# Top-32 attention without two small VectorE steps: eight entries written by GpSimd, scores three tiles ahead, operand splits spread

## The chip, the core and the metric

The kernel runs on one core of a Trainium2 chip. The time is device time in microseconds, taken from the first to the last instruction of the program; the median of several runs counts. The core has five engines that each work through their own instructions in order: TensorE (PE, with its weight loads as PEld), VectorE (DVE), ScalarE (ACT), GpSimd (POOL) and SyncE (SP), which here only issues DMAs. They wait for each other through semaphores.

## The reference

The attention has 4 x 8 heads of 576 rows and 64 columns. In each row of scores only those at or above the 32nd largest take part in the softmax:

```
scores = scale * q @ k.T                      # scale = 1/8
kth    = np.partition(scores, -32)[..., -32:-31]
scores = np.where(scores >= kth, scores, -1e9)
attn   = exp(scores - max); attn /= sum + 1e-9
out    = attn @ v
```

Its output, as 2304 tokens of 512, goes through a soft mixture of experts (`_moe_ref`: 8 experts with 4 slots each) and a top-2 mixture of experts (`_moe2_ref`: 8 experts). Both have weights of 512 x 1024 and 1024 x 512 per expert, all in float32.

## The kernel before

Two heads form a pair; there are 16 pairs. The 2 x 576 rows of a pair are nine tiles of 128 rows: four of the first head (t = 0 to 3), one with the last 64 rows of both (t = 4), four of the second head (t = 5 to 8). That makes 144 tiles. `attention` is one loop over steps `i`; in each step every engine gets one stage of several tiles, so that a tile passes through the engines over about ten steps:

- `score` (PE, then ACT): the 576 scores of each row from `QS` and `KS` into PSUM tile `S`, copied by ACT (L479) into `SS[i]`. It runs two tiles ahead of DVE's step. A pair of tiles shares one of five buffers `s`, which is ten tiles.
- `steps` (DVE): seven MAX8 over 82 columns each (L497) leave 56 candidates `C`. For the tile before, three MAX8 (L500) and two MATCH_REPLACE8 (L502) bring the 24 largest candidates into `MX`; L504 multiplies the 24th by a little less than one into `PB`.
- `count` (ACT, L517): `g`, the sign of `PB` minus the score, and its sum over the row, `SM`. So the kernel knows how many scores lie above the 24th candidate.
- `under` (POOL, L523): `u = g * s`, the scores below the bound with positive sign. Behind them `u` has nine entries that DVE writes in `fill` (L529) from `fewer`, `SM` and the 24th value: these stand for the scores above, as many as are wanted for the eighth of the following MAX8 to be the 32nd of the row.
- `pick` (DVE, L534): MAX8 over `u`; its eighth value, in `TH`, is the threshold.
- `mask` (ACT L540, then POOL L541): a relu of threshold minus score, and the row's largest minus the score, in place.
- `soft1` (PE L546, L547; ACT L553, L558): transposes of both, the second multiplied by a very large number, so that the exponential (ACT) of what is masked is zero. Every second tile also does the fifth, shared key chunk (`misc`, `et2`).
- `soft2` (PE L568, L569): the weights times `V` with a column of ones, accumulated in PSUM tile `av`. For t = 4 this runs twice with all 128 columns, once for each head. `finish` (DVE L581 to L586) divides by the sum; its pieces wait in the list `fins` and are taken between the MAX8s of the next steps.

`QS` and `KS` hold each operand as a high part, rounded to what the fast matmul takes, and a low part. For the next pair these come from `raw` (one DMA of 608 KB, `load`, L413): `split` (POOL L431, L433) makes both parts in `hl`, and `stack` lays them out in `QS` and `KS` by DMA (L437). The splits are four POOL instructions of 576 or 640 columns, one in each of four steps in a row. `raw` has two buffers, `hl` one. The first pair takes its scores straight from unsplit operands.

Table `post` names what is issued at the end of a step, `aux` (the transposes `xtr`, the `logit` and its parts, of the mixture that follows) what goes between the stages of a step. In `post` stand the loads, the stacks, and the first expert weights: five of 2 MB each at steps 40, 56, 72, 88 and 104 (`more`), and half of one at 120. Each engine's order is the order in which the program is written; SP runs ahead of the others as far as its waits let it.

After the attention the mixtures follow: matmuls on expert weights, whose buffers are filled anew as soon as the matmuls on the old content are done.

Of the kernel before, what the change touches and what calls it, by code (L numbers as in the profile page):

```python
# [8 lines left out]
F32 = mybir.dt.float32  # L9
# [9 lines left out]
UNDER = 1.0 - 2.0 ** -24  # L19
# [20 lines left out]
def moe_after_topk_attention(ctx: ExitStack, tc: tile.TileContext, q, k, v, phi, w1, w2, wg, wn, noise, u1, u2, qk, vt, out):  # L40
# [7 lines left out]
    dram = pool("dram", space=DRAM)  # L48
    wa = pool("wa")
    wz = pool("wz").tile([128, 2048], F32, name="wz")  # L50
# [36 lines left out]
    fewer = const.tile([128, 3, 4], F32, name="fewer")  # L87
    G.iota(fewer, pattern=[[-6, 3], [-2, 4]], base=528, channel_multiplier=0, allow_small_or_imprecise_dtypes=True)
    SM, PB = (const.tile([128, NT], F32, name=x) for x in ("SM", "PB"))

    TH = const.tile([128, NT + 8], F32, name="TH")
# [24 lines left out]
    def wload(i):  # L116
# [9 lines left out]
        n = 4 if m == 3 else 1  # L126
        d = WT[m, e].rearrange("p (c f) -> p c f", c=c)
        s = (w1, w2, u1, u2)[m][e].rearrange("(c p) f -> p c f", p=128)
        for a in range(n):
            cs = slice(a * c // n, (a + 1) * c // n)  # L130
            nc.sync.dma_start(d[:, cs], s[:, cs])
# [22 lines left out]
    ohw, ng = (x.rearrange("p (t e) -> p t e", e=8) for x in (TH[:, 0:NT], PB))  # L154
# [205 lines left out]
    def attention(st):  # L360
# [27 lines left out]
        RAW, HL, SP, SS, MX, G1, UU, AP, ET, E2, AV, C = ({} for _ in range(12))  # L388
        post, aux, fins, splits, cur = {}, {}, [], [], [0]
# [32 lines left out]
        def halves_of(j, a):  # L422
            splits.extend([(j, a, 0), (j, a, 1)])

        def split(j, a, l):
            if a == 0 and l == 0:
                HL[j] = tr.tile([128, 2, S + KW], F32R, name="hl")
            c = slice(S * a, S + KW * a)
            x, r = HL[j][:, :, c], RAW[j][:, c]
            if l == 0:  # L430
                G.tensor_scalar(x[:, 0], r, 1.0, 0.0, op0=OP.mult, op1=OP.add)  # L431
            else:
                G.tensor_tensor(x[:, 1], r, x[:, 0], op=OP.subtract)  # L433

        def stack(j, h):
            def move(o, i):
                nc.sync.dma_start(o.bitcast(F32), i.bitcast(F32))  # L437
            x = HL[j][64 * h:64 * h + 64]
            for l in range(2):
                o, r = QS[h][64 * l:64 * l + 64], x[:, l, 0:S]  # L440
# [5 lines left out]
            for z in range(2):  # L446
                move(KS[h][64 * z:64 * z + 64], x[:, :, S:])

        def score(i):
# [25 lines left out]
            if p is None:  # L475
                for hf in range(2):
                    A.copy(s[:, 288 * hf:288 * hf + 288], ph[hf][:, :288])
            else:
                A.copy(s.rearrange("p (a b) -> p a b", a=2), p[:, :, :288])  # L479
# [8 lines left out]
        def steps(i):  # L488
# [1040 lines left out]
```

## Time and profile before

| | us |
|---|---|
| median of 3 runs | 779.21 (779.13 to 779.62) |
| profiled execution | 783.5 |
| its span, first to last instruction | 781.6 |
| busy: PE, DVE, ACT, POOL | 755.3, 591.3, 490.3, 485.2 |

The busy times are over the whole span. Attention is the first part of it, up to about 440 us: there DVE, ACT and POOL are busy nearly all the time, and afterwards much less. A matmul's end is modelled, and the durations of neighbours on one engine overlap, so two starts in a row tell more than a duration. In the chain of work that ended last PE has 65% and DVE 22% of the span.

### The profile page before, as it was taken

Reading aid. Unit: us, or ns where it says so; the run is one execution under the profiler, and the core shown is the slowest. Engines: PE = TensorE matmul, PEld = TensorE weight load, DVE = VectorE, ACT = ScalarE, POOL = GpSimd, SP = SyncE. Lnnn points to the kernel's source line nnn. Section 1 sums busy time; section 2 is a strip of 40 time slices with the busy share of each in tenths; the row PEclk is TensorE's granted clock in tenths of the full one; section 3 lists DMA queues with packets and bytes.
Section 4 is the critical chain, followed back from the end, with each engine's and each line's share of the span. In section 5 each row is a group of like instructions: output and inputs, shape, how many; then the busy total and the mean of one; then the engine's idle time right before and its main releaser. Section 6 shows DMA issues by size and latency. Waiting matters only on the chain.

```text
span 781.6 us, 17123 instructions
## 1 busy us (share of the span) xinstructions
PE 755.3 (97%) x5623; PEld 628.0 (80%) x5623; DVE 591.3 (76%) x2916; ACT 490.3 (63%) x1019; POOL 485.2 (62%) x475
## 2 busy tenths in 40 slices
PE   9999999999999999899999999879999999999996
PEld 4799999898999889898989743356886788888884
DVE  4999999999999999889999330794654555565551
ACT  2999999999999999789998410582231322222221
POOL 3899888977898788689877200455726064273043
PEclk9999999999999999989999999898999999999998
DMA  4456878475474754755385879886955898254145
GB/s 155 115 123 169 216 196 222 89 222 136 107 213 107 186 157 97 215 129 147 65 223 205 300 279 400 274 314 214 332 157 65 291 284 188 40 67 70 16 63 68
DMA packets 62085, 135.21 MB, mean 173 GB/s; under 512 B 12450, under 2 KB 13090, under 8 KB 61986
## 3 DMA queue, kind: packets, MB, share of 16 engines
q1 hardware_dynamic: 54946, 123.83, 53.4%
q0 software_dynamic: 7040, 10.18, 9.4%
q8 instruction: 46, 0.75, 0.4%
q14 instruction: 53, 0.43, 0.2%
HBM read 84.37 MB, written 17.97 MB: 131 GB/s over the span
## 4 chain that ended last, share of the span: by engine, by line
PE 65%; DVE 22%; ACT 4%; DMA 3%; POOL 2%; issue 2%; SPq 0%; POOLq 0%; ACTq 0%; DVEq 0%
PE av L568 9%; PE acc L1286 9%; PE acc L1288 9%; PE acc L1287 9%; DVE c L497 7%; PE S L461 6%; PE st L546 4%; DVE TH L534 4%; DVE c L502 3%; PE av L569 3%; DVE mx L500 3%; PE hp L1262 2%; DMA wx<-in_moe_w_dram 2%; PE st L547 2%; PE acc L825 2%
## 5 line engine op out<-in xcount | busy, mean ns | idle before, releaser
L497 DVE MAX8 c<-s 128x8 f32<-128x82 f32 (+1 forms) x1008 | 222.9, 230 | 15.0 <-ACT s L479 7.7
L523 POOL TENSOR_TENSOR u<-g,s 128x576 f32<-128x576 bf16 x144 | 185.9, 1291 | 18.1 <-ACT g L517 11.4
L568 PE MATMUL av<-vb,et 128*128 128x65 f32 x1280 | 163.0, 271 | 0.0
L568 PEld LDWEIGHTS av<-vb,et 128*128 128x128 f32 x1280 | 159.8, 193 | 0.5 <-issue 0.4
L541 POOL TENSOR_SCALAR s<-s,mx 128x576 f32<-128x576 f32 x144 | 107.9, 749 | 55.0 <-ACT a L540 28.3
L1298 POOL DMA_INDIRECT out_dram<-y,ii x40 | 65.1, 1628 | 120.7 <-ACT y L1297 61.0
L1267 ACT ACTIVATE hh<-hp 128x640 fp32r<-128x640 f32 x62 | 43.7, 704 | 136.4 <-PE hp L1262 109.3
L1286 PE MATMUL acc<-wh,hh 128*128 128x512 f32 x320 | 127.8, 399 | 0.6 <-DVE hl L1268 0.6
L1288 PE MATMUL acc<-wh,hl 128*128 128x512 f32 x320 | 125.9, 393 | 0.0
L1287 PE MATMUL acc<-wl,hh 128*128 128x512 f32 x320 | 125.6, 393 | 0.0
L1268 DVE SCALAR_TENSOR_TENSOR hl<-hp,hh 128x640 fp32r<-128x640 f32 x62 | 51.1, 824 | 90.0 <-ACT hh L1267 89.2
L517 ACT ACTIVATE g<-s,PB 128x576 bf16<-128x576 f32 x144 | 112.6, 782 | 8.3 <-DVE PB L504 3.5
L546 PE MATMUL st<-identf,s 128*128 128x128 f32 x576 | 115.0, 280 | 1.3 <-POOL s L541 1.3
L461 PE MATMUL S<-ks,qs 128*128 128x288 f32 x600 | 114.6, 317 | 1.1 <-ACT s L479 1.1
L540 ACT ACTIVATE a<-s,TH 128x576 bf16<-128x576 f32 x144 | 114.9, 798 | 0.0
L534 DVE MAX8 TH<-u 128x8 f32<-128x585 f32 x144 | 109.4, 760 | 1.9 <-POOL u L523 1.8
L547 PE MATMUL st<-steep,a 128*128 128x128 bf16 x576 | 106.0, 220 | 0.0
L479 ACT COPY s<-S 128x576 f32<-128x576 f32 x141 | 91.4, 648 | 12.3 <-PE S L461 6.8
L461 PEld LDWEIGHTS S<-ks,qs 128*128 128x128 f32 x600 | 85.1, 191 | 9.2 <-ACT et L553 2.5
L546 PEld LDWEIGHTS st<-identf,s 128*128 128x128 f32 x576 | 84.9, 147 | 8.6 <-POOL s L541 2.2
L558 ACT ACTIVATE et<-st 128x512 f32<-128x512 f32 x144 | 85.7, 595 | 7.3 <-PE st L547 7.1
L500 DVE MAX8 mx<-c 128x8 f32<-128x56 f32 x432 | 86.3, 200 | 0.1
(341 smaller groups left out, 1263.5 us busy)
## 6 DMA issues: line engine op xcount, KB each, us to landing
wa<-in_moe_w_dram SPq DMA_DIRECT2D x11, 2048.0 KB
ks<-hl SPq DMA_DIRECT2D x60, 320.0 KB
wb<-in_moe_w_dram SPq DMA_DIRECT2D x5, 2048.0 KB
raw<-in_qk_dram SPq DMA_DIRECT2D x15, 608.0 KB
wy<-in_moe_w_dram SPq DMA_DIRECT2D x4, 2048.0 KB
wa<-in_moe_w_dram SPq DMA_DIRECT2D x16, 512.0 KB
wb<-in_moe_w_dram SPq DMA_DIRECT2D x16, 512.0 KB
vb<-in_vt_dram SPq DMA_DIRECT2D x16, 390.0 KB
```

Of the source, the lines that this page charges most:

```text
L461: T.matmul(ph[hf][:, :288], QS[h][:, q0:q0 + 128], KS[h][:, l, ks], start=(n == 0), stop=(n == len(mm) - 1))
L497: V.max(C[i][:, c * 8:c * 8 + 8], SS[i][:, cut[c]:cut[c + 1]])
L517: A.activation(g, SS[i], AF.Sign, bias=PB[:, i:i + 1], scale=-UNDER, accum_out=SM[:, i:i + 1])
L523: G.tensor_tensor(u[:, 0:S], G1[i], SS[i], op=OP.mult)
L534: V.max(thr(i, 8), UU[i])
L540: A.activation(AP[i // 2][:, S * (i % 2):S * (i % 2) + S], SS[i], AF.Relu, bias=thr(i), scale=-1.0)
L546: T.matmul(o, SP[i // 2][:, ks], identf, start=True, stop=True, is_transpose=True)
L547: T.matmul(o, AP[i // 2][:, ks], steep, start=False, stop=True, skip_group_check=True)
L568: T.matmul(o, ET[i][:, c], VB[j % 2][:, h, c], start=(c == 0), stop=False, skip_group_check=True)
L1286: T.matmul(ACC[j], HH[n][:, r], WH[n], start=(c == 0), stop=False)
L1287: T.matmul(ACC[j], HH[n][:, r], WL[n], start=False, stop=False)
L1288: T.matmul(ACC[j], HL[n][:, r], WH[n], start=False, stop=(c == 7))
```

## The change

It has eight parts, all in or around `attention`:

- L504 goes. `count` takes the 24th value itself as its bias, with a scale a little over one instead. The third MAX8 of the candidates writes its eight values straight into the table `T24`; `MX` keeps sixteen.
- L529 goes. POOL writes eight entries behind `u`, `fewer` minus `SM`, in an instruction of its own right behind `under`. These entries now are whole numbers and not multiples of the 24th value; so that they stay above or below all scores, the scores are scaled by 2 to the -40 when ACT copies them, and the exponential's scale takes it back. `pick` reads 584 columns.
- `score` runs three tiles ahead, and stands ahead of `aux` in a step.
- The splits of a pair are two instructions of 608 columns (high part) and four of 304 (low part), in six of nine steps, from 7 steps ahead of the previous pair's first tile. The low part is written over `raw`; `hl` holds the high part alone and has two buffers. The stack of `KS` takes four DMAs for a head instead of two. The stack of the first head is issued two steps earlier.
- At t = 4 `soft2` uses 64 columns of the weights for each head, on the two halves of the array (`tile_position`), into two `av` tiles that are made once and zeroed where t = 4 lies.
- `finish` is put into its list one step later, and so is `xtr`.
- The five first expert weights come in quarters of 512 KB, at steps 40 + 9i + 0, 1, 2 and 4; the half weight at step 86.
- The check of whether the fast way holds has one more condition.

```diff
-                MX[i] = wm.tile([128, 24], F32, name="mx", bufs=6)
+                MX[i] = wm.tile([128, 16], F32, name="mx", bufs=6)
...
-                    if c in (0, 2, 4):
+                    if c in (0, 2):
                         V.max(MX[k][:, c * 4:c * 4 + 8], C[k])
+                    elif c == 4:
+                        V.max(last8(T24, k), C[k])
...
-                    elif c == 5:
-                        V.tensor_scalar(PB[:, k:k + 1], MX[k][:, 23:24], UNDER, None, op0=OP.mult)
-                if 0 <= i - LP < NT:
-                    if c == CP - 2:
-                        fill(i - LP)
-                    elif c == CP:
-                        pick(i - LP)
+                if 0 <= i - LP < NT and c == CP:
+                    pick(i - LP)
...
-            A.activation(g, SS[i], AF.Sign, bias=PB[:, i:i + 1], scale=-UNDER, accum_out=SM[:, i:i + 1])
+            A.activation(g, SS[i], AF.Sign, bias=last8(T24, i, 1), scale=-OVER, accum_out=SM[:, i:i + 1])
...
-            u = UU[i] = wt.tile([128, S + 9], F32, name="u", bufs=2)
+            u = UU[i] = wt.tile([128, S + 8], F32, name="u", bufs=2)
             G.tensor_tensor(u[:, 0:S], G1[i], SS[i], op=OP.mult)
+            G.tensor_tensor(u[:, S:S + 8], fewer, SM[:, i:i + 1].to_broadcast([128, 8]), op=OP.subtract)
...
-                A.copy(s.rearrange("p (a b) -> p a b", a=2), p[:, :, :288])
+                A.activation(s.rearrange("p (a b) -> p a b", a=2), p[:, :, :288], AF.Copy, scale=TINY)
...
-                HL[j] = tr.tile([128, 2, S + KW], F32R, name="hl")
...
+                HL[j] = tr.tile([128, W], F32R, name="hl", bufs=2)
+            f = slice(a * W // n, (a + 1) * W // n)
+            r, x = RAW[j][:, f], HL[j][:, f]
             if l == 0:
+                G.tensor_scalar(x, r, 1.0, 0.0, op0=OP.mult, op1=OP.add)
             else:
+                G.tensor_tensor(r.bitcast(F32R), r, x, op=OP.subtract)
...
             for z in range(2):
-                move(KS[h][64 * z:64 * z + 64], x[:, :, S:])
+                for l in range(2):
+                    move(KS[h][64 * z:64 * z + 64, l], x[l][:, S:])
...
+            hs = [(0, 4, 64, 0), (1, 4, 64, 64)] if t == 4 else [(0, t, 128, 0)] if t < 4 else [(1, t - 5, 128, 0)]
+            for c in range(5):
+                for h, tt, m, o in hs:
+                    x = ET[i][:, c, o:o + m] if c < 4 else E2[i // 2][:, o:o + m]
+                    T.matmul(av[h][o:o + m, tt * 65:tt * 65 + 65], x, VB[j % 2][:, h, c if c < 4 else 4 + i % 2],
+                             start=(c == 0), stop=(c == 4), tile_position=(0, o), skip_group_check=True)
...
+                for n, x in zip((-7, -6, -4, -3, -1, 0), ((0, 0, 2), (1, 0, 4), (1, 1, 4), (0, 1, 2), (1, 2, 4), (1, 3, 4))):
...
-                at(t0 + 5, stack, j + 1, 0)
-                at(t0 + 7, stack, j + 1, 1)
+                at(t0 + 3 if j else 0, stack, j + 1, 0)
+                at(t0 + 7 if j else 1, stack, j + 1, 1)
...
-            at(40 + 16 * i, more, i + 1)
-        at(120, whalf, 0, wz)
+            for a in range(4):
+                at(40 + 9 * i + (0, 1, 2, 4)[a], wload, i, a)
+        wnext[0] = 5
+        at(86, whalf, 0, wz)
...
+            if i + 3 < NT:
+                score(i + 3)
...
-            if i + 2 < NT:
-                score(i + 2)
```

DVE, one step without a finish, before; `c` are candidates, `s` scores, `mx` the largest candidates:

```order
L500 MAX mx_825<-c_826 128x8
L497 MAX c_871<-s2_816 128x8
L502 MATCH_REPLACE c_826<-mx_825,c_826 128x56
L529 TENSOR_SCALAR u_793<-fewer_101,SM_103,mx_717 128x9
L497 MAX c_871<-s2_816 128x8
L500 MAX mx_825<-c_826 128x8
L497 MAX c_871<-s2_816 128x8
L504 TENSOR_SCALAR PB_104<-mx_825 128x1
L534 MAX TH_105<-u_793 128x8
L497 MAX c_871<-s2_816 128x8
```

And the same piece of a step of DVE in the changed kernel:

```order
L502 MAX mx_885<-c_886 128x8
L499 MAX c_938<-s2_769 128x8
L506 MATCH_REPLACE c_886<-mx_885,c_886 128x56
L499 MAX c_938<-s2_769 128x8
L504 MAX T24_105<-c_886 128x8
L499 MAX c_938<-s2_769 128x8
L530 MAX TH_104<-u_859 128x8
L499 MAX c_938<-s2_769 128x8
```

Both TENSOR_SCALARs are gone; the pick follows the sixth MAX8 directly.

POOL, two steps with splits, before; `hl` and `raw` are the operands of the next pair:

```order
L523 TENSOR_TENSOR u_2590<-g_2588,s2_2442 128x576
L431 TENSOR_SCALAR hl_2612<-raw_2131 128x576
L541 TENSOR_SCALAR s1_2338<-s1_2338,mx_2397 128x576
L523 TENSOR_TENSOR u_2643<-g_2641,s2_2442 128x576
L433 TENSOR_TENSOR hl_2612<-raw_2131,hl_2612 128x576
```

And two steps of POOL with splits in the changed kernel, where L522 is `under` and L537 the subtraction of `mask`:

```order
L522 TENSOR_TENSOR u_1722<-g_1720,s4_1511 128x576
L523 TENSOR_TENSOR u_1722<-fewer_101,SM_103 128x8
L432 TENSOR_SCALAR hl_1743<-raw_1637 128x608
L537 TENSOR_SCALAR s3_1412<-s3_1412,mx_1528 128x576
L522 TENSOR_TENSOR u_1770<-g_1768,s4_1511 128x576
L523 TENSOR_TENSOR u_1770<-fewer_101,SM_103 128x8
L434 TENSOR_TENSOR raw_1637<-raw_1637,hl_1743 128x304
```

Each `under` is followed by an instruction over eight columns; a low part takes 304 columns and is written over `raw`.

SP's queue from the load of `V` to the load of the next `raw`, before:

```order
L420 DMA vb1_199<-in_vt_dram 128x780
L437 DMA qs1_193<-hl_1141 64x512
L437 DMA qs1_193<-hl_1141 64x64
L437 DMA qs1_193<-hl_1141 64x512
L437 DMA qs1_193<-hl_1141 64x64
L437 DMA ks1_195<-hl_1141 64x2x640 x2
L590 DMA out_0_dram<-xr_126 128x512
L413 DMA raw_1636<-in_qk_dram 128x1216
```

The same stretch of SP's queue in the changed kernel; the `raw` loaded in its last row lies in the buffer of the `raw` that the rows before read:

```order
L422 DMA vb0_198<-in_vt_dram 128x780
L438 DMA qs1_193<-hl_377 64x512
L438 DMA qs1_193<-hl_377 64x64
L438 DMA qs1_193<-raw_312 64x512
L438 DMA qs1_193<-raw_312 64x64
L438 DMA ks1_195<-hl_377 64x640
L438 DMA ks1_195<-raw_312 64x640
L438 DMA ks1_195<-hl_377 64x640
L438 DMA ks1_195<-raw_312 64x640
L585 DMA out_0_dram<-xr_126 128x512
L415 DMA raw_1153<-in_qk_dram 128x1216
```

Two DMAs more lie ahead of the load, and half of them read `raw` itself.

## Rows read from the trace of the kernel before

**Rows 1.** Instructions of line L534: duration min/median/max in ns, first and last start

```profile
L534 DVE MAX8 TH<-u x144: 748/759/774, 19.1 to 432.3; 128x8 f32<-128x585 f32 x144
```

**Rows 2.** Stretches, line L534 alone: length, DVE busy (count), PE clock, DMA share, GB/s

```profile
43.58:145.80 102.22, 27.37 (x37) 1.00 0.71 184
```

**Rows 3.** Stretches: length, busy us (count) of PE, PEld, DVE, ACT, POOL

```profile
43.58:145.80 102.22, 99.64 (x908) 94.76 (x908) 101.84 (x643) 95.99 (x208) 89.18 (x89) 1.00 0.71 184
```

**Rows 4.** Chain that ended last, after attention: start us, us, what

```profile
465.48 17.05 DMA wx<-in_moe_w_dram
```

**Rows 5.** Timeline of DVE: start us, us, instruction, tiles, shapes

```profile
113.99 0.27 DVE L529 TENSOR_SCALAR u<-fewer,SM,mx 128x9 f32<-128x9 f32 x1
114.18 0.23 DVE L497 MAX8 c<-s 128x8 f32<-128x82 f32 x1
...
114.59 0.13 DVE L504 TENSOR_SCALAR PB<-mx 128x1 f32<-128x1 f32 x1
114.65 0.75 DVE L534 MAX8 TH<-u 128x8 f32<-128x585 f32 x1
```

**Rows 6.** Timeline of ACT, two tiles apart

```profile
203.88 0.60 ACT L558 ACTIVATE et<-st 128x512 f32<-128x512 f32 x1
...
208.91 0.64 ACT L558 ACTIVATE et<-st 128x512 f32<-128x512 f32 x1
```

**Rows 7.** Groups of the page, ACT: busy us, mean ns | idle before

```profile
L479 ACT COPY s<-S 128x576 f32<-128x576 f32 x141 | 91.4, 648 | 12.3 <-PE S L461 6.8
...
L558 ACT ACTIVATE et<-st 128x512 f32<-128x512 f32 x144 | 85.7, 595 | 7.3 <-PE st L547 7.1
```

**Rows 8.** Timeline of POOL, a stretch without gaps

```profile
40.79 1.42 POOL L433 TENSOR_TENSOR hl<-raw,hl 128x576 fp32r<-128x576 f32 x1
42.18 0.77 POOL L541 TENSOR_SCALAR s<-s,mx 128x576 f32<-128x576 f32 x1
42.89 1.31 POOL L523 TENSOR_TENSOR u<-g,s 128x576 f32<-128x576 bf16 x1
44.14 0.75 POOL L431 TENSOR_SCALAR hl<-raw 128x640 fp32r<-128x640 f32 x1
```

**Rows 9.** Groups by shape, POOL's small instructions

```profile
L1047 POOL TENSOR_TENSOR wx<-LT,g 128x96 f32<-128x96 f32 x1 | 0.4, 424 | 22.5 <-DVE wx L1151 22.5
...
L79 POOL IOTA cap<- 128x8 f32 x1 | 0.1, 128 | 0.0
```

**Rows 10.** Timeline of PE around three tiles

```profile
181.48 0.22 PE L547 MATMUL st<-steep,a 128*128 128x128 bf16 x1
181.63 1.07 PE L247 MATMUL misc<-xl,xt 128*32 128x512 f32 x8
...
182.98 0.80 PE L461 MATMUL S<-ks,qs 128*128 128x288 f32 x4
...
185.31 0.22 PE L547 MATMUL st<-steep,a 128*128 128x128 bf16 x1
185.33 0.78 PE L461 MATMUL S<-ks,qs 128*128 128x288 f32 x4
...
196.21 1.06 PE L568 MATMUL av<-vb,et 128*128 128x65 f32 x8
...
197.32 0.28 PE L546 MATMUL st<-identf,s 128*128 128x128 f32 x1
```

**Rows 11.** Timeline of SP's queue: start us, us to issue, DMA

```profile
1.68 0.43 SPq L413 DMA_DIRECT2D raw<-in_qk_dram  x1
...
309.88 1.06 SPq L131 DMA_DIRECT2D wx<-in_moe_w_dram  x1
...
315.77 1.28 SPq L437 DMA_DIRECT2D ks<-hl  x2
```

**Rows 12.** Timeline of POOL, its waits for DMAs, [idle before <-releaser]

```profile
7.16 0.68 POOL L431 TENSOR_SCALAR hl<-raw 128x576 fp32r<-128x576 f32 x1 [4.30 <-DMA raw<-in_qk_dram]
...
327.35 0.67 POOL L431 TENSOR_SCALAR hl<-raw 128x576 fp32r<-128x576 f32 x1 [4.34 <-DMA ks<-hl]
```

More of the change, by code (lines that the diff above doesn't have):

```diff
@@ L85, in moe_after_topk_attention @@
            allow_small_or_imprecise_dtypes=True)
[L87 to L91, printed above, removed]
+    fewer = const.tile([128, 8], F32, name="fewer")
+    G.iota(fewer, pattern=[[-2, 8]], base=528, channel_multiplier=0, allow_small_or_imprecise_dtypes=True)
+    SM = const.tile([128, NT], F32, name="SM")
+    TH, T24 = (const.tile([128, NT + 8], F32, name=x) for x in ("TH", "T24"))
     wgn = const.tile([128, 4, 16], F32, name="wgn")
@@ L114, in whalf, with wload @@
             "(c p) f -> p c f", p=128))
-    def wload(i):
+    def wload(i, part=None):
         m, e = order[i]
@@ L125, in wload @@
         c = 4 if m % 2 == 0 else 8
-        n = 4 if m == 3 else 1
+        n = 4 if m == 3 or part is not None else 1
         d = WT[m, e].rearrange("p (c f) -> p c f", c=c)
         s = (w1, w2, u1, u2)[m][e].rearrange("(c p) f -> p c f", p=128)
-        for a in range(n):
+        for a in range(n) if part is None else [part]:
             cs = slice(a * c // n, (a + 1) * c // n)
@@ L387, in attention @@
         V.memset(empty.rearrange("p (j f) -> p j f", f=ROW)[:, :, NS:NS + 1], 4096.0)
-        RAW, HL, SP, SS, MX, G1, UU, AP, ET, E2, AV, C = ({} for _ in range(12))
-        post, aux, fins, splits, cur = {}, {}, [], [], [0]
+        RAW, HL, SP, SS, MX, G1, UU, AP, ET, E2, C = ({} for _ in range(11))
+        av = [ps.tile([128, 512], F32, name=f"av{h}", bufs=1) for h in range(2)]
+        post, aux, fins, splits, cur = {}, {}, [], {}, [0]
         def row():
@@ L539, in mask @@
                 AP[i // 2] = ap[i // 2 % 2].tile([128, 2 * S], BF, name=f"a{i // 2 % 2}")
-            A.activation(AP[i // 2][:, S * (i % 2):S * (i % 2) + S], SS[i], AF.Relu, bias=thr(i), scale=-1.0)
+            A.activation(AP[i // 2][:, S * (i % 2):S * (i % 2) + S], SS[i], AF.Relu, bias=last8(TH, i, 1), scale=-1.0)
             G.tensor_scalar(SS[i], SS[i], -1.0, MX[i][:, 0:1], op0=OP.mult, op1=OP.add)
@@ L552, in soft1 @@
                 masked(p[:, :128], 512)
-                A.activation(e2, p[:, :128], AF.Exp, scale=-0.125)
+                A.activation(e2, p[:, :128], AF.Exp, scale=-0.125 / TINY)
             p = ps.tile([128, 512], F32, name="st", bufs=2)
@@ L602, in attention @@
         load(1)
+        for a in av:
+            V.memset(a[:, 260:325], 0.0)
         p = ps.tile([128, 512], F32, name="misc", bufs=2)
@@ L613, in attention @@
         warm(2)
+        score(2)
+        warm(2)
         LK, LP, LM, LS, CP = 1, 3, 4, 5, 5
@@ L665, in attention @@
                 f(*z)
-            if i + 2 < NT:
-                score(i + 2)
-                if i < 6:
-                    warm(2)
-            if splits:
-                split(*splits.pop(0))
+            if i in splits:
+                split(*splits[i])
             if 0 <= i - LS - 1 < NT:
```

69 lines of the change are left out of this document (29 added, 40 removed).

## The prediction

> **What bounds the kernel now.** I read the page first, then the starts of one instruction, then three stretches. The instruction is `pick` (L534), which runs once for each of the 144 tiles of scores: its first start is 19.1 us and its last 432.3 us [rows 1], so 143 tiles take 413.2 us, 2.89 us each. This is where all edits lie. The second view cuts out 43.58 to 145.80 us, from the pick of tile 9 to that of tile 45: 37 picks, so 36 tiles, in 102.22 us, 2.84 us each [rows 2]. DVE is busy 101.84 of them [rows 3]; ACT has 95.99, POOL 89.18 (durations overlap, so a busy share flatters all of them, PE most). The reader should see that DVE never waits here and sets the pace. The third view is the start to start spacing on each engine where it runs without a gap, since that, and not the duration, is what an instruction costs in a row.
>
> After attention nothing that is edited is on the path. The next long piece of the chain is the wait for expert weights, 17.05 us from 465.48 [rows 4]; those transfers go into buffers that matmuls after the attention set free. They move with its end, so I count what attention saves one for one.
>
> **The change part by part.**
>
> *DVE loses two instructions a tile.* L529 starts at 113.99 and its successor at 114.18: 0.19 us. L504 starts at 114.59, its successor at 114.65: 0.06 us [rows 5]. Together 0.25 us, so DVE's own pace goes from 2.84 to 2.59 us. Taken alone, 144 x 0.25 = 36 us. `pick` reads 584 instead of 585 values, which is nothing. That all 36 us show needs the other three engines to be faster than 2.59, and that has to be read from them.
>
> *ACT.* Between 203.88 and 208.91 ACT has no gap and finishes two tiles: 5.03 us, 2.52 each [rows 6]. The copy of the scores becomes an activation with a scale. The nearest row is the exponential out of PSUM, 595 ns for 512 columns, which is 669 for 576 by proportion, against 648 for the copy [rows 7]: +0.02. From below it is nothing, from above I bound it by what 64 more columns would add, 0.07; I take 0.02, since the exponential reads the same kind of memory and has no per-partition bias either. The copy of a transposed x, 512 columns, comes once in nine tiles, by L479's 648 ns for 576 about 0.06 a tile. ACT: 2.60.
>
> *POOL gets the eight entries behind u, and other splits.* Where POOL has no gap, L541 costs 42.18 to 42.89, 0.71, and L523 42.89 to 44.14, 1.25 [rows 8]: 1.96 a tile. A pair's splits were four instructions; they are now two of 608 columns (by L431, 0.75 for 640, about 0.71 each) and four of 304 (L433 takes 1.39 for 576 from 40.79 to 42.18; half of that is 0.73, and a fixed part makes it about 0.78): 4.5 us in nine tiles, 0.50 a tile, what it was before within a few hundredths. The new TENSOR_TENSOR over 8 columns has no row. From below: an iota over 8 columns, 0.13. From above: a TENSOR_TENSOR over 96, 0.42 [rows 9]. I take 0.15, near the iota, since L433's 576 columns in 1.39 leave little that does not scale with the columns. POOL: 2.61. It had cover before (89.18 of 102.22), and now has none; at 0.42 it would be 2.88.
>
> *PE.* A tile without the fifth key chunk takes 182.98 to 185.33, 2.35 us [rows 10]; every second tile has two more matmuls, and a pair has a second score group at tile 4 and the transposes of x; for these I put 0.2 a tile on top (an estimate, with 0.1 of it for each). At tile 4 two groups of ten matmuls ran after each other, the second from 196.21 to 197.32, 1.11 us [rows 10]. They become pairs of 64 columns on the two halves of the array. That such column groups run side by side is in the trace: eight matmuls of 512 columns at L247, in four groups, take 1.07 us in all. I expect about 1.0 us less in nine tiles, 0.11 a tile; from below nothing saved, if halves take turns. The second group is 0.12 a tile now, so PE stands at 2.67 and would come to 2.56; with nothing saved it stays at 2.67. The logits and weighings, once in four pairs, are not in it.
>
> The Trainium skill, TensorEngine Tiling, Key Properties, speaks against this piece: changing the tiling mode drains TensorE. The trace agrees: L547 starts at 181.48, and L247, the first that is split into column groups, follows 0.15 us later; behind the L547 at 185.31, L461 on the whole array follows after 0.02 [rows 10]. By that rule each pair pays perhaps 0.2 us, 3 us in sixteen pairs, for some 16 gained; without it 16. My sum takes the saving as 0.11 a tile either way, because PE is not the highest of the four.
>
> *Scores three tiles ahead, `aux` behind the score.* DVE has one more tile in stock when PE is held by a logit or a weighing. Only the excess of the mean, 2.89, over DVE's pace, 2.84, can be paid for by it: 0.05 x 143 = 7 us, of which the next edit takes the most.
>
> *The halves `hl` in two buffers, splits earlier.* POOL stood 4.34 us at 327.35 because the split needed `hl` while the copies out of it (`ks<-hl`, issued 315.77, behind 2 MB of weights issued 309.88) had not landed [rows 11, 12]. With two buffers that wait goes, and weights come in quarters. What is late next: `raw`. It is now overwritten by the low half, so the load of the next pair into it waits until the stacking DMAs have read it; there are six to eight of these (two more than before for each head), 0.64 us each on SP (ks x2 in 1.28). The load takes about 5.5 us (issued 1.68, POOL released 7.16) [rows 11, 12]. The first split of that pair stands two tiles after the load's place in the program, where it was eight. I count from SP's release, about five and a half tiles before the split: 5.6 us of issues, 2.5 to land (estimate), 5.5 for the load, 13.6, against 5.5 x 2.6 = 14.3 us. It fits barely. In the first pair POOL will stand about 1 us. I count 1 us in all, and bound it by 11.6 us (327.35 minus 315.77) in place of 2.5 on five pairs with weights ahead of them, about 40 us.
>
> *Finishes a tile later; memsets of av, `fewer`, check.* DVE's reads of `av` come later than PE's last write, at no cost; the check's extra DVE instruction lies beside matmuls that wait for weights.
>
> **The sum.** After the change the four engines stand at 2.59 (DVE), 2.60 (ACT), 2.61 (POOL) and 2.56 (PE). With one clear leader the mean lay 0.05 over its pace, and more than half of that was the 4.34 us stall. With four within 0.1 us, a step that is long on one (a split of 0.78 us, DVE's finishes, PE's logits) meets no slower engine that hides it; a stock of about two tiles takes some of it. I allow 0.12 a tile, between 0 and 0.23 (where nearly all is lost): 2.73 x 143 = 390.4 us instead of 413.2, 22.8 saved, minus the 1 us of raw: 22. The profiled execution takes 783.5 us, its span is 781.6, and the median of the timed runs is 779.2, 2.4 below the span. 781.6 - 22 - 2.4 = 757 us.
>
> **The rivals.**
>
> *The gain goes whole.* The engines' stock is enough: 2.61 x 143 = 373, 40 saved, 5 given back to logits: 35, 744 us. For: ACT alone held 2.52 for two tiles with the others in step. Against: four would have to do so for nine tiles.
>
> *Another engine takes over.* The small POOL instruction costs 0.3 instead of 0.15, or the array's halves take turns and the drains come on top: the leader stands at 2.75, plus 0.08: 2.83, 8 saved, 771 us. At 0.42 on POOL it is 2.88 and nothing is left. For: POOL has no row for this instruction, and 96 columns cost 0.42. Against: the 8-column iota.
>
> *Slower: POOL waits for `raw` in each pair.* Place: the first split of a pair, two tiles after its load; behind it on POOL stand L541 (PE waits for it) and L523 (DVE's pick). Fourteen loads; the gain of 22 us is gone from 1.6 us of waiting per load that no stock absorbs. At 2.5 us: 35 lost, 13 slower, 792 us. For: the 11.6 us that a landing took behind 2 MB. Against: weights are in 512 KB pieces, three of the four issued right behind the first stack, five tiles before.
>
> *It does not do what it says:* score copies three ahead have ten tiles of room, and the buffer that a copy takes was freed one tile before; if PE's transposes of that tile were late, ACT would wait each second tile. PE runs these transposes before the score in its own order, so I give this nothing of its own.
>
> **How the numbers follow.** Forecast 757: 0.58. Whole gain, 744: 0.12. Another engine, 771: 0.17, with 0.04 more for no change. Slower: 0.09. Faster by over 0.2% (1.6 us, about what a measurement of this kernel can tell from no change) takes the first three, 0.87; within it 0.04; slower 0.09. The range reaches from 744, the floor with four engines at 2.61, to 772, which takes in the other engine's case and leaves the slower one out.
>
> **What would show it.** The starts of `pick` should lie 2.7 us apart in the mean, with 2.4 in tiles that have no finish. POOL's busy time in that stretch should come to over 95% and DVE should now have waits. The 8-column instruction should show 0.13 to 0.2 us; the matmuls of tile 4 pairs that start together. The stall near 327 us should be gone. Waits of POOL for `raw<-in_qk_dram` of over 1.6 us in most pairs, or an 8-column instruction of 0.4, would make the forecast wrong.

## The result, and the profile after

The changed kernel takes 758.25 us, the median of 4 runs (757.15 to 761.49), against 779.17 us (777.77 to 779.62) for the kernel before in runs on the same chip: a ratio of 0.974 with a 95% interval of 0.971 to 0.978. The forecast was 757 us. The profiled execution takes 757.15 us and its span is 755.4 us (before 783.5 and 781.6).

All of it lies in attention. `pick` is now L530, and its instructions answer to [rows 1]:

```profile
L530 DVE MAX8 TH<-u x144: 740/755/773, 14.5 to 406.8; 128x8 f32<-128x584 f32 x144
```

The first and the last start are 392.3 us apart, 2.74 us a tile, against 2.89. Behind the last pick the span still has 348.6 us (349.3 before): the tail moved one for one.

The first pick comes 4.6 us earlier (14.5 instead of 19.1 us). That is no part of the change that can be counted on: among the fourteen profiled kernels of this study the first pick starts between 13.3 and 14.5 us in eleven and between 18.9 and 19.8 us in three, and two of them that are the same program up to there (experiments 10 and 12) fall on either side; the last section shows what the three have in common. Where two traces are compared below I therefore use a measure without the start, the time from the fifteenth pick to the last, 129 tiles, worked out from the starts of `pick`: 374.1 us before and 352.4 after, 21.6 us less, where the medians differ by 20.9.

The stretches of the changed kernel, from pick to pick, answer to [rows 2, 3]; columns as there (length, busy us and count of PE, PEld, DVE, ACT and POOL, granted clock, DMA share, GB/s). The first row is three pairs, the others one pair each:

```profile
54.39:125.76 71.37, 70.21 (x682) 66.64 (x680) 70.20 (x427) 70.91 (x157) 71.37 (x100) 1.00 0.78 207
125.76:149.53 23.77, 23.28 (x228) 22.08 (x226) 23.37 (x142) 23.48 (x53) 23.77 (x34) 1.00 0.80 214
149.53:175.24 25.71, 25.70 (x247) 23.10 (x247) 24.40 (x145) 24.38 (x57) 23.94 (x34) 1.00 0.72 196
175.24:201.16 25.92, 25.92 (x248) 22.77 (x247) 23.71 (x142) 25.24 (x56) 23.92 (x34) 1.00 0.70 197
```

The same picks, one pair or more per row, in the kernel before:

```profile
58.20:134.87 76.67, 74.77 (x683) 71.07 (x681) 76.39 (x483) 71.86 (x154) 67.05 (x67) 1.00 0.76 201
134.87:161.31 26.44, 25.59 (x231) 23.07 (x230) 26.21 (x163) 24.51 (x54) 21.63 (x22) 1.00 0.50 105
161.31:213.42 52.11, 52.11 (x484) 48.33 (x483) 51.27 (x323) 49.60 (x110) 44.70 (x44) 1.00 0.60 156
```

The first row says who sets the pace now: POOL, busy 71.37 of 71.37 us, at 2.64 us a tile (DVE before: 2.84). The third and fourth row hold a logit and what follows it, and there PE is the one without a gap, at 25.7 to 25.9 us a pair. So the change gains 1.77 us in a pair without such work (25.56 to 23.79), and 3.2 us in the three pairs around the logit (26.44 + 52.11 against 23.77 + 51.63). The later pairs show the same two levels.

POOL in the quiet part, answering to [rows 8, 9]; L522 is `under`, L523 the eight entries, L537 the subtraction of `mask`:

```profile
65.89 1.28 POOL L522 TENSOR_TENSOR u<-g,s 128x576 f32<-128x576 bf16 x1
67.14 0.19 POOL L523 TENSOR_TENSOR u<-fewer,SM 128x8 f32<-128x8 f32 x1
67.31 0.69 POOL L432 TENSOR_SCALAR hl<-raw 128x608 fp32r<-128x608 f32 x1
67.99 0.74 POOL L537 TENSOR_SCALAR s<-s,mx 128x576 f32<-128x576 f32 x1
...
69.95 0.19 POOL L523 TENSOR_TENSOR u<-fewer,SM 128x8 f32<-128x8 f32 x1
70.11 0.82 POOL L434 TENSOR_TENSOR raw<-raw,hl 128x304 fp32r<-128x304 f32 x1
70.92 0.74 POOL L537 TENSOR_SCALAR s<-s,mx 128x576 f32<-128x576 f32 x1
```

From start to start `under` costs 1.25, the eight entries 0.16 to 0.17, the high part 0.68, the low part 0.81, the subtraction 0.71 us. Nine tiles come to 9 x 2.13 + 2 x 0.68 + 4 x 0.81 = 23.77 us, and a quiet pair takes 23.77 to 23.80: POOL's instructions stand one behind the other.

PE at tile 4, answering to [rows 10]:

```profile
63.03 0.27 PE L214 MATMUL misc<-identf,xl 64*128 64x64 f32 x1
63.23 0.80 PE L563 MATMUL av<-vb,et 128*64 128x65 f32 x20
63.96 0.33 PE L542 MATMUL misc<-identf,s 128*128 128x128 f32 x1
```

Twenty matmuls of 64 columns take 0.73 us to the next start, where the two groups of ten took 1.06 and 1.11 us one after the other.

What waits for what, answering to [rows 12]; columns: who waits <- for whom, us in all, times, longest:

```profile
DVE TH L530 <- POOL u L523: 17.8, 34, 1.8
POOL s L537 <- ACT a L536: 14.3, 22, 1.5
...
POOL hl L432 <- DMA raw<-in_qk_dram: 2.7, 1, 2.7
```

DVE, which before had waited 9.8 us in all between 15 and 440 us, now waits 17.8 us for POOL's eight entries alone; POOL waits for `raw` once (until 19.1 us). No split waits for `hl`, and the pair with the 4.34 us stall, 30.14 us long, takes 23.79 now.

The one wait for `raw` has a tail. Behind it PE is idle from 19.9 to 22.8 us, and from 22.9 to 29.7 us the granted clock is 0.50 (the level of 1.2 GHz). The kernel of experiment 8, whose first pick comes at the same 14.5 us, has neither this wait nor the pause of PE and stays at 1.00. The same stretch, changed kernel first, experiment 8 second:

```profile
22.90:29.70 6.80, 6.80 (x30) 4.94 (x30) 5.77 (x37) 3.62 (x8) 5.90 (x8) 0.50 0.28 94
```

```profile
22.90:29.70 6.80, 6.80 (x63) 6.53 (x63) 6.80 (x44) 6.80 (x17) 6.03 (x10) 1.00 0.27 92
```

PE gets through half as many matmuls, and from the first pick to the fifteenth the changed kernel takes 39.9 us, experiment 8 36.4; how much of that is the wait, the clock or the other place of the splits there is not separated. The old stall had such a tail as well: PE idle from 326.0 to 328.8 us, then a granted clock of 0.50 from 330.2 to 337.0. In the changed kernel the granted clock is 1.00 from 29.7 us to the end of attention.

### The profile page after: what moved, and what is told of

Same layout as the page of the kernel before. It is cut to its first block, busy times and chain, and to the rows that moved or that the text cites. A ratio compares the mean times of both kernels' runs of the same rounds, so it can differ in the third digit from the quotient of the medians.

```text
span 755.4 us, 17253 instructions
## 1 busy us (share of the span) xinstructions
PE 728.6 (96%) x5623; PEld 601.6 (80%) x5623; DVE 559.0 (74%) x2631; ACT 485.7 (64%) x1019; POOL 511.2 (68%) x649
## 4 chain that ended last, share of the span: by engine, by line
PE 53%; DVE 23%; POOL 12%; issue 6%; DMA 3%; ACT 2%; SPq 0%; POOLq 0%; DVEq 0%; ACTq 0%
PE acc L1289 9%; PE acc L1291 9%; PE acc L1290 9%; DVE c L499 9%; PE av L563 5%; POOL u L522 5%; DVE TH L530 4%; DVE c L506 3%; PE S L463 3%; POOL s L537 3%; PE st L542 3%; PE hp L1265 2%; DMA wx<-in_moe_w_dram 2%; DVE mx L502 2%; PE acc L828 2%
## 5 line engine op out<-in xcount | busy, mean ns | idle before, releaser
L522 POOL TENSOR_TENSOR u<-g,s 128x576 f32<-128x576 bf16 x144 | 186.4, 1294 | 0.7 <-ACT g L516 0.7
L563 PE MATMUL av<-vb,et 128*128 128x65 f32 (+1 forms) x1600 | 172.5, 262 | 0.8 <-ACT et L549 0.8
L563 PEld LDWEIGHTS av<-vb,et 128*128 128x128 f32 (+1 forms) x1600 | 165.9, 181 | 7.8 <-issue 5.3
L537 POOL TENSOR_SCALAR s<-s,mx 128x576 f32<-128x576 f32 x144 | 108.0, 750 | 22.5 <-ACT a L536 14.3
L530 DVE MAX8 TH<-u 128x8 f32<-128x584 f32 x144 | 109.2, 759 | 18.6 <-POOL u L523 17.8
L536 ACT ACTIVATE a<-s,TH 128x576 bf16<-128x576 f32 x144 | 117.9, 818 | 0.2
L516 ACT ACTIVATE g<-s,T 128x576 bf16<-128x576 f32 x144 | 116.9, 812 | 0.4 <-POOL u L522 0.4
L481 ACT ACTIVATE s<-S 128x576 f32<-128x576 f32 x141 | 97.3, 690 | 6.7 <-PE S L470 4.6
L542 PEld LDWEIGHTS st<-identf,s 128*128 128x128 f32 x576 | 84.2, 146 | 13.3 <-POOL s L537 6.4
L554 ACT ACTIVATE et<-st 128x512 f32<-128x512 f32 x144 | 90.9, 631 | 5.6 <-PE st L543 4.9
L1289 PEld LDWEIGHTS acc<-wh,hh 128*128 128x128 f32 x320 | 60.7, 190 | 14.4 <-issue 2.7
## 6 DMA issues: line engine op xcount, KB each, us to landing
wa<-in_moe_w_dram SPq DMA_DIRECT2D x8, 2048.0 KB, 12.4
```

Source lines behind the costliest of these rows:

```text
L516: A.activation(g, SS[i], AF.Sign, bias=last8(T24, i, 1), scale=-OVER, accum_out=SM[:, i:i + 1])
L522: G.tensor_tensor(u[:, 0:S], G1[i], SS[i], op=OP.mult)
L530: V.max(last8(TH, i), UU[i])
L536: A.activation(AP[i // 2][:, S * (i % 2):S * (i % 2) + S], SS[i], AF.Relu, bias=last8(TH, i, 1), scale=-1.0)
L537: G.tensor_scalar(SS[i], SS[i], -1.0, MX[i][:, 0:1], op0=OP.mult, op1=OP.add)
L542: T.matmul(o, SP[i // 2][:, ks], identf, start=True, stop=True, is_transpose=True)
```

## The experiments

The experiments ran in three groups, each with its own runs of the kernel before (medians 780.37, 779.71 and 780.69 us); a ratio, with its 95% interval, is against these runs and need not be the quotient of the two medians. The medians can tell some 2 to 4 us; the 129 tiles (374.1 before, 352.4 changed) come from one execution each, without the start. What they leave out, the first pick to the fifteenth, takes 35.9 to 45.2 us in the fourteen kernels; the three longest (experiments 1, 3 and 12, over 44 us) have a granted clock of 0.50 for 14 to 17 us there, the two shortest (6 and 8) none.

**1. The eight entries written twice** (changed kernel).

```diff
             G.tensor_tensor(u[:, S:S + 8], fewer, SM[:, i:i + 1].to_broadcast([128, 8]), op=OP.subtract)
+            G.tensor_tensor(u[:, S:S + 8], fewer, SM[:, i:i + 1].to_broadcast([128, 8]), op=OP.subtract)
```

> The eight-column instruction on POOL runs twice for each tile (it writes the same values again). Theory A, POOL sets the pace in the pairs without logits (71.37 of 71.37 us busy in the stretch 54.39 to 125.76, 2.64 us a tile) and PE in the pairs with them: 0.157 us more for each of about 84 tiles, 13 us, and what is beyond POOL's slack in the others: 771 us, 769 to 778. Theory B, DVE still sets the pace and POOL is only busy because it is kept busy: 758 to 760 us.

787.3 us, ratio 1.006 [1.003, 1.009]; 129 tiles 378.5 us. POOL in this kernel, two tiles:

```profile
70.13 0.21 POOL L523 TENSOR_TENSOR u<-fewer,SM 128x8 f32<-128x8 f32 x1
70.43 0.20 POOL L524 TENSOR_TENSOR u<-fewer,SM 128x8 f32<-128x8 f32 x1
70.61 0.75 POOL L538 TENSOR_SCALAR s<-s,mx 128x576 f32<-128x576 f32 x1
71.32 1.30 POOL L522 TENSOR_TENSOR u<-g,s 128x576 f32<-128x576 bf16 x1
```

Theory A has the sign right and the size wrong: with a second write to the same entries behind it the instruction costs 0.27 to 0.30 instead of 0.16 us, and both together 0.46 in the median, 0.48 in these rows. That is 0.29 to 0.31 more a tile, and a quiet pair takes 26.39 us, 2.6 or 9 x 0.29 more: whatever POOL spends shows one for one. Whether the same entries make the first write dearer, or any short instruction behind a short one, was not separated. The median is 29 us over the changed kernel, the 129 tiles 26.

**2. One small DVE instruction more** (changed kernel; its result is not read).

```diff
                 if 0 <= i - LP < NT and c == CP:
+                    V.tensor_scalar(idle[:, 0:1], last8(T24, i - LP, 1), 1.0, None, op0=OP.mult)
                     pick(i - LP)
```

> DVE gets one instruction of one column more for each tile, ahead of the pick, whose result nobody reads. Its cost by L504 of the kernel before is about 0.05 us. Theory A (POOL sets the pace at 2.64 us, DVE stands at about 2.59): DVE comes to 2.64, still not above POOL: 758 to 761 us. Theory B (DVE sets it): 0.05 x 144 = 7 us more, 765 to 767 us.

760.43 us, ratio 0.974 [0.969, 0.979], that of the changed kernel; 129 tiles 353.1 us, 0.7 more. DVE has room.

**3. The eight entries written by DVE** (changed kernel otherwise).

```diff
-            G.tensor_tensor(u[:, S:S + 8], fewer, SM[:, i:i + 1].to_broadcast([128, 8]), op=OP.subtract)
...
+                if 0 <= i - LP < NT and c == CP - 2:
+                    V.tensor_tensor(UU[i - LP][:, S:S + 8], fewer, SM[:, i - LP:i - LP + 1].to_broadcast([128, 8]), op=OP.subtract)
```

> The eight entries behind u are written by one DVE instruction instead of the POOL one, where L529 stood before; the other dropped DVE step stays dropped. Theory A: POOL falls to 2.48 us a tile, DVE rises from 2.59 by 0.1 to 0.19 and becomes the bound at 2.69 to 2.78: 4 to 12 us slower in the quiet pairs, some in the others, 768 us, 762 to 774. Theory B (DVE sets the pace already): 14 to 27 us slower, 772 to 785 us. Theory C, that the gain has little to do with the dropped DVE steps and comes from the order (scores ahead, splits, weights): within 2 us of 758.

780.03 us, ratio 0.999 [0.995, 1.003]: the whole gain is gone, more than theory A had; 129 tiles 370.7 us, 3.3 less than before, with 5.3 us more than the changed kernel from the first pick to the fifteenth. The number lies in theory B's range, but experiment 2 and the waits of DVE above say that DVE did not set the pace in the changed kernel. A quiet pair is back at 25.5 us, and DVE is busy 71.22 of 71.50 us. DVE in this kernel, at two tiles:

```profile
67.61 0.60 DVE L531 TENSOR_TENSOR u<-fewer,SM 128x8 f32<-128x8 f32 x1
68.13 0.23 DVE L499 MAX8 c<-s 128x8 f32<-128x82 f32 x1
...
70.54 0.30 DVE L531 TENSOR_TENSOR u<-fewer,SM 128x8 f32<-128x8 f32 x1
70.77 0.23 DVE L499 MAX8 c<-s 128x8 f32<-128x82 f32 x1
```

And POOL at the same time:

```profile
66.89 1.29 POOL L525 TENSOR_TENSOR u<-g,s 128x576 f32<-128x576 bf16 x1
...
69.53 1.29 POOL L525 TENSOR_TENSOR u<-g,s 128x576 f32<-128x576 bf16 x1
70.79 0.71 POOL L432 TENSOR_SCALAR hl<-raw 128x608 fp32r<-128x608 f32 x1
```

Eight columns take DVE 0.52 us once and 0.23 the next time, and each time they are done when POOL's running instruction ends (66.89 + 1.29 = 68.18, and 70.79, where POOL's next one begins). Over all 144 the mean from start to start is 0.30 us (0.26 in the quiet stretch), where theory A had 0.10 to 0.19; of the fifteen that fell into a pause of POOL fourteen took 0.07. The TENSOR_SCALAR that stood here before took 0.19 [rows 5]. The Trainium skill, SBUF — State Buffer, on who interferes with whom, says that a DVE instruction with two inputs in SBUF and a GpSimd instruction that reads SBUF exclude each other, and that the later one waits for the whole instruction of the earlier; this trace agrees. So the new form of the entries pays only off DVE. The old TENSOR_SCALAR with only L504 dropped was not run.

**4. The DVE drop alone** (kernel before, with T24, the scaled scores and POOL's eight entries; scores, splits, t = 4, finishes and weights as before).

```diff
+                    elif c == 4:
+                        V.max(last8(T24, k), C[k])
...
-                    elif c == 5:
-                        V.tensor_scalar(PB[:, k:k + 1], MX[k][:, 23:24], UNDER, None, op0=OP.mult)
-                if 0 <= i - LP < NT:
-                    if c == CP - 2:
-                        fill(i - LP)
...
+            G.tensor_tensor(u[:, S:S + 8], fewer, SM[:, i:i + 1].to_broadcast([128, 8]), op=OP.subtract)
```

> The kernel before with the two DVE steps dropped as in the change (scaled scores, eight entries by POOL) and nothing else: scores two ahead, splits as before in four steps, tile 4 with whole columns, weights in 2 MB pieces. Theory A: DVE, POOL and PE stand at 2.59, 2.61 and 2.67 us, the stall near 327 us stays and logits hit a stock of one tile: about half of the gain, 768 us, 763 to 772. Theory B (DVE alone counts): 779 - 0.25 x 143 = 743 us. Theory C: 777 to 781 us.

779.13 us, ratio 0.998 [0.995, 1.0004]; 129 tiles 373.3 us, 0.8 less than before. Theory A, and with it my step on DVE, missed. Three quiet pairs of this kernel in one stretch:

```profile
52.98:127.54 74.56, 72.93 (x679) 70.45 (x679) 71.29 (x428) 71.25 (x155) 70.71 (x94) 1.00 0.78 207
```

DVE is down to 71.29, as it should be, and no engine is busy throughout: quiet pairs take 24.56 and 25.44 us by turns. Where they lose it can be seen on POOL, around a pair's splits (L434 low part, L432 high part, L521 `under`):

```profile
60.16 1.29 POOL L521 TENSOR_TENSOR u<-g,s 128x576 f32<-128x576 bf16 x1
61.40 0.21 POOL L522 TENSOR_TENSOR u<-fewer,SM 128x8 f32<-128x8 f32 x1
61.56 1.42 POOL L434 TENSOR_TENSOR hl<-raw,hl 128x576 fp32r<-128x576 f32 x1
62.95 0.77 POOL L536 TENSOR_SCALAR s<-s,mx 128x576 f32<-128x576 f32 x1
63.66 1.31 POOL L521 TENSOR_TENSOR u<-g,s 128x576 f32<-128x576 bf16 x1
...
66.51 1.31 POOL L521 TENSOR_TENSOR u<-g,s 128x576 f32<-128x576 bf16 x1
...
70.17 1.31 POOL L521 TENSOR_TENSOR u<-g,s 128x576 f32<-128x576 bf16 x1
```

Three tiles in a row take POOL 3.50, 2.85 and 3.66 us. In the pairs with a logit (27.2 to 27.5 us, 26.4 to 26.6 before) and at the stall (31.6 us, 30.1 before) it gives back what it gained.

**5. Everything but the drop** (changed kernel with both DVE instructions back; the reverse of 4).

> The counterpart of drop_alone: all of the change but the two dropped DVE steps, which stand as before (L504, and L529 with nine entries on DVE, scores unscaled). Theory A (drop and order need each other: DVE at 2.84 us a tile bounds all pairs without logits as before): only the stall near 327 us and part of the logits' excess go, 772 us, 769 to 776. Theory C (the order alone brings the gain): 757 to 762 us.

771.03 us, ratio 0.989 [0.984, 0.994]; 129 tiles 366.4 us, 7.6 less than before. Quiet pairs take 25.55 us, exactly what they took before, and DVE is busy 76.37 of 76.66 us there. What it gains is the stall (30.14 to 25.56 us) and 0.9 to 1.5 us in the three pairs around each logit. 0.8 for the one half, 7.6 for the other, and 21.6 for both (1.2, 8.7 and 20.9 by the medians): 11 to 13 us exist only together.

**6. Scores two tiles ahead** (changed kernel, `aux` ahead of the score again).

```diff
-        score(2)
...
-            if i + 3 < NT:
-                score(i + 3)
...
             if i in aux:
...
+            if i + 2 < NT:
+                score(i + 2)
```

> The changed kernel with scores two tiles ahead again and aux ahead of the score, as before. Theory A (with four engines within 0.1 us a tile, the stock of one more tile is what lets them run at POOL's 2.64): pairs without logits lose 0.3 to 1 us each, the six with logits 1 to 2 us: 769 us, 763 to 778. Theory D (spread splits alone even out POOL, the stock is not needed): 758 to 761 us.

757.4 us, ratio 0.971 [0.967, 0.975]; 129 tiles 351.5 us, 0.9 less than the changed kernel. Theory D holds: the third tile in stock is worth nothing here.

**7. t = 4 as before** (changed kernel otherwise).

```diff
-            hs = [(0, 4, 64, 0), (1, 4, 64, 64)] if t == 4 else ...
-            for c in range(5):
-                for h, tt, m, o in hs:
+            hs = [(0, 4, 128, 0), (1, 4, 128, 0)] if t == 4 else ...
+            for h, tt, m, o in hs:
+                for c in range(5):
```

> The changed kernel with tile 4 as before, ten matmuls of 128 columns for each of two heads one after the other. Theory A: about 1.06 us more on PE in each pair; in six pairs with logits PE is the bound and 6 us show, in the others PE comes to 2.67, just over POOL's 2.64, 2 us: 766 us, 762 to 771. Theory D (PE is not the bound anywhere): 758 to 760 us.

770.51 us, ratio 0.988 [0.984, 0.994]; 129 tiles 364.8 us, 12.4 more than the changed kernel. Three quiet pairs:

```profile
52.90:126.10 73.20, 73.16 (x681) 70.87 (x681) 70.69 (x428) 70.79 (x157) 71.53 (x101) 1.00 0.76 201
```

PE is the one without a gap now, and a pair takes 24.4 us: 2.71 a tile, 0.6 us a pair over POOL. In the pairs with a logit and behind it, where PE is the bound anyway, it is 0.8 to 1.6 us a pair.

**8. The splits in four steps in a row** (changed kernel otherwise).

```diff
-                for n, x in zip((-7, -6, -4, -3, -1, 0), ((0, 0, 2), (1, 0, 4), (1, 1, 4), (0, 1, 2), (1, 2, 4), (1, 3, 4))):
+                for n, x in zip((0, 1, 2, 3), ((0, 0, 2), (1, 0, 2), (0, 1, 2), (1, 1, 2))):
...
-                at(t0 + 3 if j else 0, stack, j + 1, 0)
+                at(t0 + 5 if j else 0, stack, j + 1, 0)
```

> The changed kernel with the splits in four steps in a row (high 608, low 608, high 608, low 608) and the first stack two steps later, as before; hl keeps its two buffers. POOL has 0.3 us less to do in a pair (two low instructions of 608 in place of four of 304), but in those four tiles it needs 2.12 + 1.07 = 3.2 us each. Theory A (what kept drop_alone from gaining is mainly that POOL cannot hide four long tiles in a row): 770 us, 764 to 777. Theory E (the stock of scores covers it, and only the sum of POOL's work counts): 755 to 759 us.

765.95 us, ratio 0.983 [0.977, 0.988], 7.7 us more than the changed kernel; 129 tiles 364.5 us, 12.1 more, of which the first tiles give 3.5 back (no wait for `raw`, no fall of the clock). The four larger instructions cost POOL 0.3 us a pair less than the six, and yet a quiet pair takes 24.4 to 24.9 us and one with a logit up to 28.4: bunching is what costs. The edit also brings the splits and the first stack later; PE's waits for `ks` show that with 2.1 us in four, a small part.

**9. The drop and t = 4, without the spread splits** (kernel before, with the edits of 4 and the halves of t = 4).

> The kernel before with two parts of the change: the two DVE steps dropped, and tile 4 on the halves of the array. Scores two ahead, splits in four steps in a row from one buffer of hl, weights in 2 MB pieces. Theory A (drop_alone gained nothing because PE, 2.71 us a tile with whole columns, and POOL's four long tiles take turns at the bound): with PE relieved the pairs without logits fall to about 24.5 us, the stall near 327 us stays: 771 us, 767 to 775. Theory F (POOL's bunched splits alone hold it): no gain over drop_alone, 777 to 780 us.

775.35 us, ratio 0.992 [0.989, 0.994], between theory A and theory F; 129 tiles 368.4 us. Quiet pairs still take 24.55 and 25.48 us, as in 4. Three of them come to 74.59 us, three in experiment 8 to 74.47: with the splits in a row, the parts of the change that 8 has beyond 9 (two buffers of `hl`, scores three ahead, weights in smaller pieces, later finishes) make no difference there. With 4, 7 and 8: the drop pays in full only when PE's tile 4 is shortened and POOL's splits are spread as well.

**10. The low part in two pieces of 608 columns, still spread** (changed kernel otherwise).

```diff
-                for n, x in zip((-7, -6, -4, -3, -1, 0), ((0, 0, 2), (1, 0, 4), (1, 1, 4), (0, 1, 2), (1, 2, 4), (1, 3, 4))):
+                for n, x in zip((-7, -5, -3, -1), ((0, 0, 2), (1, 0, 2), (0, 1, 2), (1, 1, 2))):
```

> The changed kernel with the low parts in two POOL instructions of 608 columns in place of four of 304, two steps apart from the high ones (7, 5, 3 and 1 steps ahead of the pair before). An instruction of 304 took 0.82 us, one of 608 about 1.47: 0.33 us less in a pair, 2.61 us a tile for POOL in place of 2.64. Theory A (POOL sets the pace in the pairs without logits, and ten of sixteen are such): 755 us, 753 to 758. Theory G (an instruction of 1.47 us makes its tile too long, and the others wait): 758 to 764 us.

761.17 us, ratio 0.973 [0.968, 0.978]; 129 tiles 353.5 us. The four splits now cost POOL 0.3 us a pair less, and a quiet pair takes 23.7 to 23.9 us as ever: theory G. Three quiet pairs:

```profile
59.65:131.00 71.35, 69.74 (x680) 66.45 (x679) 70.20 (x427) 70.29 (x155) 70.77 (x94) 1.00 0.78 206
```

Now POOL too has pauses, and all four stand within about a microsecond of each other: here the interleaving costs what an allowance is for. Which instruction the others wait for was not followed.

**11. The logits in four column groups** instead of two (changed kernel otherwise).

```diff
-                for h in range(2):
-                    T.matmul(p[32 * h:32 * h + 32, :288], phs[:, hp, :], XT[b * 4 + hp][:, h * 288:h * 288 + 288],
+                for h in range(4):
+                    T.matmul(p[32 * h:32 * h + 32, :144], phs[:, hp, :], XT[b * 4 + hp][:, h * 144:h * 144 + 144],
```

> The changed kernel with the logits of a batch in four column groups of 144 columns in place of two of 288 (sixteen matmuls in the place of eight, half as long, and four copies by ACT in place of two). The block took 2.06 us on PE; it should take about 1.1. Theory A (PE is the bound where the logits lie): 1 us less in each of three batches, 755 us, 753 to 758. Rival: the copies or DVE's reduction behind the logits hold that stretch: 758 to 760 us.

756.46 us, ratio 0.969 [0.965, 0.974]; 129 tiles 350.4 us, 2.1 less than the changed kernel. The piece on PE, changed kernel first, this kernel second:

```profile
149.71 1.17 PE L221 MATMUL misc<-xt,phs 128*32 128x288 f32 x8
...
151.77 0.43 PE L563 MATMUL av<-vb,et 128*128 128x65 f32 x2
```

```profile
148.77 0.70 PE L221 MATMUL misc<-xt,phs 128*32 128x144 f32 x16
...
149.88 1.33 PE L563 MATMUL av<-vb,et 128*128 128x65 f32 x10
```

2.06 us become 1.11, and the three pairs with a logit become 0.6 to 0.7 us shorter: PE is the bound there. The median's gain over the changed kernel, 1.8 us, is within what the runs can tell.

**12. Edits 10 and 11 together.**

> low_in_two and logit_four together in the changed kernel. Theory A: 752 us, 750 to 757. If either hurts as its rival says: 758 to 764 us.

758.62 us, ratio 0.970 [0.966, 0.974]; 129 tiles 351.5 us. No gain over the changed kernel. No version of this study beats it by more than the runs can tell; 11 comes nearest.

## Why the prediction was right, point by point

**What bounds, and the four paces: right.** DVE was the bound and POOL is the next one, as the sum had it: 2.64 us a tile for 2.61. The eight entries cost 0.16 to 0.17 for 0.15, and experiment 1 shows that every tenth of a microsecond on this engine counts. PE with whole tiles at t = 4 stands at 2.71 (experiment 7) for 2.67. ACT takes 5.21 us for two tiles where it has no gap, 2.60 each, the forecast's value. These are the starts of two instructions two tiles apart:

```profile
100.22 0.86 ACT L536 ACTIVATE a<-s,TH 128x576 bf16<-128x576 f32 x1
...
105.43 0.77 ACT L536 ACTIVATE a<-s,TH 128x576 bf16<-128x576 f32 x1
```

The signs came as well: in the quiet pairs four tiles of nine have picks 2.41 us apart (2.4 forecast for tiles without a finish), and the matmuls at tile 4 start in pairs.

**The allowance of 0.12 a tile: right in size, wrong in what it stands for.** The mean is 2.74 for a forecast of 2.73. But in the quiet pairs nothing is lost in interleaving: 23.79 us is POOL's own time. The 0.10 between the mean and POOL's pace lies in the six pairs with or behind a logit, at 25.7 to 26.2 us, 2.2 us above a quiet one each (13 us), and in the first tiles. I had left the logits out of PE's pace and put an allowance over all tiles instead. That the left-out term is about as large as the allowance, and that 0.03 too little on POOL nearly cancels 0.02 too much in the allowance, is luck: the closeness of 757 to 758 owes something to it. A better sum takes the pairs of each kind by themselves.

**The drop's price taken alone: on a condition that did not hold.** The text priced the drop at 36 us if taken alone and the other three engines faster than 2.59; the three were not, and they were not because of parts that other edits remove. The drop alone is worth 0.8 us (experiment 4), the rest alone 7.6. The sum over all edits came out since it was made for the four engines after all edits.

**t = 4: right in kind, too small.** About 1.0 us a pair was forecast. Two groups took 1.06 + 1.11 = 2.2; the twenty now take 0.73, and the step into them up to 0.2 us (63.03 to 63.23): about 1.2 saved. The drain at a change of tiling that the Trainium skill, TensorEngine Tiling, Key Properties, names is no larger than that in this trace. I said that the sum would not depend on it, "because PE is not the highest of the four"; experiment 7 shows that it does: without it PE is the highest, and 12 us are gone. The rival in which another engine takes over had 771 us for this case; it measured 770.5.

**Scores three ahead: worth nothing** (experiment 6), for a part of the 7 us that the text put on this and the next edit together. Two tiles in stock are enough here.

**`hl` and `raw`: right, and cheaper than the upper bound.** The stall is gone, `raw` makes POOL wait once, 2.7 us (1 us forecast), and the rival that ended slower had its price at each pair: it did not come. The 2.5 us for a stack's DMA to land, for which the text had no row, were 2.2 to 6.0 in the changed kernel (median about 3); the load lands 2.2 us or more before its first split in every later pair. What the sum did not have is the fall of the clock behind the one wait, which comes on top of it. Which of the two edits removed the stall, the second `hl` or the quartered weights, was not separated.

**Splits: the missing term.** I priced their durations and not their places. Spread over nine steps they keep POOL's longest tile near 3 us; in four steps in a row the same work costs 8 us of the whole time, 12 in the 129 tiles (experiment 8).

Experiments 10 and 12 had slower first tiles in their profiled execution (from the sixth pick to the fifteenth 26.1 and 28.7 us, 24.2 in the changed kernel). The granted clock goes with it: 0.50 from 30.6 to 37.4 us in 10 and from 21.0 to 38.1 in 12, where it is 0.50 from 22.9 to 29.7 in the changed kernel, each time at or right behind a pause of PE (28.2 to 29.7, 19.3 to 22.0 and 19.9 to 22.8 us).

Still open: whether the place of that pause belongs to the edits or to the execution. The finishes a step later, the weights in smaller pieces and the second `hl` were not run by themselves.

## What to carry to other kernels

When four engines stand within a few per cent of each other, a cheaper step on the leader pays nothing by itself: write down every engine's pace after all edits, and for each kind of stretch apart, and look for the edits that only pay together. What an engine does once in a while has to be spread over the loop in small pieces; its place can cost more than a saving in its length brings.

## What the runs showed of the hardware

- On POOL the eight-column instruction costs 0.16 us from start to start behind a long one, but 0.27 to 0.30 when the next instruction is a second write to the same entries (experiment 1).
- An eight-column instruction of DVE with two inputs takes 0.07 us when POOL pauses (fourteen of fifteen), and otherwise mostly ends with POOL's running instruction, up to 0.5 us later in the rows shown (experiment 3).
- Matmuls of 64 columns on the two halves of the array run side by side with their weight loads: twenty in 0.73 us.
- The start of the program has two forms, and TensorE's clock tells them apart. The trace's list of granted clocks begins with an entry of 1.00 (the level of 2.4 GHz) at 19.6, 19.8 and 20.3 us in the three kernels whose first pick comes late (before, experiments 6 and 10), and between 3.8 and 5.8 us in the other eleven. Ahead of that entry a stretch's row prints 1.00 for want of an entry, and is no reading: matmuls of 288 columns start 0.48 us apart there and 0.24 us behind it, and 0.48 again where the granted clock is 0.50. Experiments 10 and 12 are the same program up to the first logit. Experiment 10 first, 12 second:

```profile
5.00:12.00 7.00, 6.97 (x13) 3.08 (x14) 3.17 (x21) 1.64 (x4) 3.76 (x4) 1.00 0.64 190
```

```profile
5.00:12.00 7.00, 6.80 (x28) 3.00 (x28) 5.11 (x38) 3.51 (x8) 3.73 (x4) 1.00 0.66 203
```

The same four matmuls on PE, experiment 10 ahead of its first entry and behind it:

```profile
14.54 2.29 PE L470 MATMUL S<-xr 64*128 64x288 f32 x4
...
20.66 1.24 PE L470 MATMUL S<-xr 64*128 64x288 f32 x4
```

Why the rise comes so late in three is open. The first pick moves by 5 us with it (19.8 and 14.0), which is why one profile's span alone proves no gain of that size.
